# Plain float32 operands for the first token block's MLP in a fused attention, MLP and expert kernel

## The chip, the cores and the metric

One core of one Trainium2 chip runs the whole program. The metric is the device time of one execution in microseconds. Engines are named as in the profile: PE multiplies, PEld is its weight load, DVE, ACT and POOL work element by element, SP issues the transfers.

## What is computed

The reference joins three layers (cut to what matters):

```
x  = attention(q, k, v)                  # 4 x 8 heads, 576 positions, 64 features; a coarse and a banded part
h  = x @ w_in                            # 2304 x 512 @ 512 x 2048
g  = maximum(h, 0) + log1p(exp(-abs(h)))
y  = g @ w_out                           # 2048 x 512
e  = argmax(y @ w_gate + modality_bias)  # one of 8 experts for each token
out = gate * (maximum(y @ w1[e], 0) @ w2[e])
```

All of it is float32 in the reference; `w_in` and `w_out` arrive as float64 bits. The change concerns the lines of `h`, `g` and `y` for the first 384 of 2304 tokens.

## The kernel before

The tokens are cut into six blocks of 384 (`TB`, `NB`). For each block the MLP goes over 16 chunks of 128 hidden features: `mlp_H` multiplies a chunk of `w_in` by the block's x (line 557), three ACT instructions and line 572 on DVE make g, and `mlp_Y` multiplies g by a chunk of `w_out` into four PSUM banks that are held for the whole block (line 588). After the six blocks the same blocks pass through the experts (lines 557 and 632).

A product is made of float32r operands in two parts, `hi` and `lo = value - hi`: `hi*hi + hi*lo + lo*hi`, three matmuls. So every operand is split: a piece of a weight by `split` (lines 464 and 465: a copy on ACT, a subtraction on POOL), x by lines 354 and 355, g by lines 573 and 574. In block 0 line 573 runs on ACT and line 574 on POOL; in the blocks after it both run on DVE.

The weights are converted from float64 bits only once, while block 0 runs: `from_f64` takes a piece of 128 x 512 through line 425 on ACT and lines 426 to 429 on DVE. There are 32 pieces, 16 of `w_in` and 16 of `w_out`; the raw bits arrive by DMA in six buffers, and SP issues a new transfer when line 429 has freed one. The attention is written in steps that are interleaved with the MLP: what block 1 needs is made while block 0 is multiplied. Its matmuls (lines 167, 208, 237, 247, 304, 329, 338) take plain float32 operands.

The order on each engine comes from a scheduler that goes by its own estimate of the times; each engine then works through its instructions strictly in that order. So an instruction on DVE that takes longer than another also holds back what stands behind it, g above all, and PE waits for g in its second product.

Of the kernel before, what the change touches and what calls it, by code (L numbers as in the profile page):

```python
# [25 lines left out]
TB = 384  # L26
# [11 lines left out]
MASKED = -1.0e9  # L38
# The float64 2.0 ** -127 has the high word 0x38000000: as a float32, this.
F64_LEAST = 2.0 ** -15  # L40
# [6 lines left out]
C0 = 3  # L47
CR = 1


@with_exitstack
def band_attention__softplus_mlp__top1_moe(
# [49 lines left out]
    def ahead(n):  # L102
        """The scheduler takes what is emitted inside as if it had been n instructions earlier."""
        return tc.high_priority(n) if n else nullcontext()
# [7 lines left out]

# [1 line left out]
    xT = {}  # L114
    od = {}

    class Down:
# [37 lines left out]
        def trans(self, i):  # L155
            """q or k of both heads, features on partitions."""
            t = apool.tile([128, S], F32, tag=("qT", "kT")[i], name="qkT", bufs=4)
            half = RT // 2
            for g in range(2):
                ps = pa("pT")  # L160
                for r in range(half):
                    if self.b < 0:
                        for h in range(2):
                            T.matmul(ps[h * D:(h + 1) * D, r * RP:(r + 1) * RP], self.raw[i][:, h, g * half + r, :],
                                     ident[:RP, :RP], start=True, stop=True)
                        continue
                    T.transpose(ps[:, r * RP:(r + 1) * RP], self.raw[i][:, g * half + r].rearrange("p h d -> p (h d)"),  # L167
                                ident[:RP, :RP])
                warm(ps)
                o = t.rearrange("m (p r) -> m r p", r=RT)[:, g * half:(g + 1) * half, :]  # L170
                x = ps[:, :half * RP].rearrange("m (r p) -> m r p", r=half)
                if i == 0:
                    A.mul(o, x, SCALE) if g or nloc[0] >= 12 else V.tensor_scalar(o, x, SCALE, None, ALU.mult)
                else:
                    (A.copy if nloc[0] < 16 else V.tensor_copy)(o, x)
            return t
# [82 lines left out]
    def warm(ps):  # L259
        """Keeps the tensor engine's clock up while the attention leaves it idle; nobody reads the columns."""  # L260
        if 4 <= nloc[0] < 12:
            for i in range(1):
                T.matmul(ps[:, 384:384 + 128], ident, ident[:, :128], start=True, stop=True)

    def pa(name):
        """A bank for the attention: while the MLP has not begun, of any of the three pools."""
        if not started[0]:
            nps[0] += 1
            if nps[0] % 2:
                return psy.tile([128, 512], F32, tag="py", name=name)  # L270
        return psa.tile([128, 512], F32, tag="pa", name=name)
# [3 lines left out]
    class Local:  # L275
# [58 lines left out]
        def st_PV(self):  # L334
# [8 lines left out]
            if blk not in xT:  # L343
                xT[blk] = xpool.tile([128, 2, CC, TB], F32R, tag="xT", name="xT")
            xf = apool.tile([128, TH // FACTOR, FACTOR], F32, tag="xf", name="xf", bufs=2)
            jd = self.j * (TH // FACTOR)
            odb = od[self.b][:, self.hp, jd:jd + TH // FACTOR].rearrange("p (g o) -> p g o", o=1)
            V.tensor_tensor(
                out=xf, in0=ps[:, :TH].rearrange("p (g r) -> p g r", r=FACTOR),
                in1=odb.to_broadcast([128, TH // FACTOR, FACTOR]), op=ALU.add)  # L350
            xf = xf.rearrange("p g r -> p (g r)")
            hi = xT[blk][:, 0, self.hp, off:off + TH]
# [21 lines left out]
    def load_after(n):  # L374
        """The loads that fit once job n has been transposed."""
        while loads and loads[0][0] <= n:
# [40 lines left out]

# [1 line left out]
    def from_f64(raw, dst, on_g):  # L419
        """float64 bits, as (low, high) pairs of int32, to float32: the exponent loses its three  # L420
        redundant bits, the mantissa is cut to 23 bits, and what is under float32's range ends under
        its least normal number, as zero does."""
        lo, hi = raw[:, :, 0], raw[:, :, 1]
# [45 lines left out]

    def split_wi(n, c):  # L470
        wis[n, c] = split(wi[:, c] if n < NB else mo["w1"][:, :, c * 128:(c + 1) * 128], "wis")

    def split_wo(n, c):
        wos[n, c] = split((wo if n < NB else mo["w2"])[:, c, :], "wos")

    load_after(-3)

# [1 line left out]
    def router_setup():  # L479
# [19 lines left out]
    def router(n):  # L499
        """Each quarter of the features has its own columns of the array; the sum over them comes after the transpose."""  # L500
        ps = psa.tile([128, 512], F32, tag="pa", name="pR")
# [30 lines left out]
    def count_others():  # L532
        """How many tokens chose each expert but the first token's, and how many in all."""
        hits = const.tile([128, E, NTT], F32, name="hits")
# [11 lines left out]

# [1 line left out]
    gst = {}  # L548
    yps = {}

    def mlp_H(n, c):
        ps = psa.tile([128, 512], F32, tag="pa", name="ph")
        wt = wis.pop((n, c))
        i = 0
        for cc in range(CC):
            for w, x in ((0, 0), (0, 1), (1, 0)):
                T.matmul(ps[:, :TB], wt[:, w, cc, :], xT[n][:, x, cc, :], start=(i == 0), stop=(i == 3 * CC - 1))  # L557
# [9 lines left out]

    def mlp_g(n, c):
        g = mlp.tile([128, 2, TB], F32R, tag="g", name="g", bufs=3)
        if n < NB:  # L570
# [10 lines left out]
    def mlp_Y(n, c):  # L581
        g, w = gst.pop((n, c)), wos.pop((n, c))
        if c == 0:
            yps[n] = [psy.tile([128, 512], F32, tag="py", name="py") for _ in range(CC)]
        for dc in range(CC):
            dsl = slice(dc * 128, (dc + 1) * 128)
            for i, (a, b) in enumerate(((0, 0), (0, 1), (1, 0))):
                T.matmul(yps[n][dc][:, :TB], w[:, a, dsl], g[:, b, :], start=(c == 0 and i == 0),  # L588
# [9 lines left out]

# [1 line left out]
    mo = {}  # L600

    def load_expert(e):
        """One expert's weights."""
        for h in range(2):
# [8 lines left out]
    def load_y(n, y=None):  # L613
        """Block n's MLP output, split, as the experts' operand."""
        if y is None:
# [7 lines left out]
    def moe_Y(n, cs, mask=None):  # L623
        """The second product for chunks cs, token tile by token tile."""
        gw = [(gst.pop((n, c)), wos.pop((n, c))) for c in cs]
# [30 lines left out]

# [1 line left out]
    if 0:  # L658
# [63 lines left out]

# [1 line left out]
    # So far every token went through the first token's expert. What chose another one is computed  # L724
    # again: for each such expert all blocks, of which its tokens' rows are kept.
    with tc.If(nc.values_load(todo[0:1, E:E + 1], min_val=0, max_val=NT) > 0):
# [48 lines left out]
```

## Time and profile before

| what | value |
|---|---|
| runs | 836.1, 836.75, 838.21 us; median 836.75 |
| profiled execution | span 836.3 us from the first to the last instruction; no other time of it is listed |
| PE busy | 789.5 us of the span, 94% |
| DVE, ACT, POOL busy | 512.4, 476.7, 522.5 us |
| mean granted clock of TensorE | 0.962 of full |

The span is read in stages. Up to about 64 us the attention of the first tokens is made and nothing of the MLP runs. Block 0's first product begins at 64.4 us. The conversions end at 196.6 us, block 0's last product at about 213.5 us, and from there on PE has hardly a gap.

### The profile page before, as it was taken

What the parts mean: (1) busy time and instruction counts of PE and PEld (TensorE: products, weight loads), DVE (VectorE), ACT (ScalarE), POOL (GpSimd) and SP (SyncE); (2) the same over time, 40 slices, a digit from 0 to 9 for tenths busy, and PEclk for the clock granted to TensorE, in tenths of its full rate; (3) what the DMA queues carried; (4) which work ended last, traced back from release to release, by engine and by line L of the source; (5) the groups of instructions that cost most, each with busy time, mean ns of one, the idle gap of its engine ahead of it and who ended that gap; (6) DMA issues with size and microseconds to landing.
All of it is one profiled execution on the core that took longest, in us unless ns stands there. A gap on an engine that the chain in (4) does not pass through costs nothing.

```text
span 836.3 us, 14455 instructions
## 1 busy us (share of the span) xinstructions
PE 789.5 (94%) x5229; PEld 718.9 (86%) x5230; DVE 512.4 (61%) x1011; ACT 476.7 (57%) x1206; POOL 522.5 (62%) x491
## 2 busy tenths in 40 slices
PE   5997887888999999999999999999999999999996
PEld 4776876776989998898989999999998899999995
DVE  6879999998597576677765566638561512222121
ACT  5756775665556664657755665646663444444342
POOL 3457757668566575666656666656666666666662
PEclk9868988989999999999999999999999999999999
DMA  9936554432220041021100010036011102001011
GB/s 171 199 84 149 175 174 127 137 100 55 74 64 5 15 113 43 13 62 39 36 1 12 11 49 1 2 110 242 1 36 42 63 14 76 1 38 38 1 39 41
DMA packets 82169, 55.49 MB, mean 66 GB/s; under 512 B 61081, under 2 KB 73899, under 8 KB 82091
## 3 DMA queue, kind: packets, MB, share of 16 engines
q1 hardware_dynamic: 82091, 54.50, 23.4%
q8 instruction: 43, 0.70, 0.3%
q14 instruction: 35, 0.29, 0.1%
HBM read 45.05 MB, written 9.44 MB: 65 GB/s over the span
## 4 chain that ended last, share of the span: by engine, by line
PE 74%; DVE 17%; ACT 3%; issue 3%; SPq 1%; DMA 1%; DVEq 0%; ACTq 0%
PE ph L557 31%; PE py L588 19%; PE py L632 12%; DVE cva L428 3%; DVE cva L427 3%; PE pO L338 2%; PE pS L304 2%; DVE cva L426 2%; PE pA L329 2%; PE pT L167 1%; DVE ga L572 1%; PE pO L247 1%; PE pA L237 1%; DVE g L573 1%; PE pS L208 1%
## 5 line engine op out<-in xcount | busy, mean ns | idle before, releaser
L557 PE MATMUL ph<-xT,wis 128*128 128x384 f32 x1152 | 234.9, 352 | 8.2 <-DVE ls L310 2.6
L588 PE MATMUL py<-g,wos 128*128 128x384 f32 x1152 | 233.8, 345 | 2.4 <-ACT g L573 1.0
L557 PEld LDWEIGHTS ph<-xT,wis 128*128 128x128 f32 x1152 | 208.5, 197 | 13.1 <-ACT cva L425 2.7
L588 PEld LDWEIGHTS py<-g,wos 128*128 128x128 f32 x1152 | 199.7, 190 | 9.3 <-issue 2.5
L465 POOL TENSOR_TENSOR wis<-wi,wis 128x512 fp32r<-128x512 f32 x96 | 129.0, 1344 | 71.0 <-ACT wis L464 62.2
L465 POOL TENSOR_TENSOR wos<-wo,wos 128x512 fp32r<-128x512 f32 x96 | 132.4, 1380 | 48.2 <-ACT wos L464 47.9
L557 PE MATMUL ph<-yT,wis 128*128 128x384 f32 x576 | 108.2, 336 | 0.0
L578 DVE SCALAR_TENSOR_TENSOR g<-ph,g 128x384 fp32r<-128x384 f32 x48 | 26.7, 557 | 131.2 <-ACT g L577 131.2
L632 PE MATMUL py<-wos,g 128*128 128x512 f32 x432 | 106.6, 392 | 0.0
L557 PEld LDWEIGHTS ph<-yT,wis 128*128 128x128 f32 x576 | 101.5, 188 | 3.5
L465 POOL TENSOR_TENSOR wos<-w2s,wos 128x512 fp32r<-128x512 f32 x48 | 63.9, 1332 | 49.4 <-ACT wos L464 49.4
L632 PEld LDWEIGHTS py<-wos,g 128*128 128x128 f32 x432 | 80.3, 188 | 15.3 <-ACT wis L464 0.6
L563 ACT ACTIVATE ga<-ph 128x384 f32<-128x384 f32 x96 | 46.7, 487 | 78.1 <-PE ph L557 76.6
L572 DVE SCALAR_TENSOR_TENSOR ga<-ph,ga 128x384 f32<-128x384 f32 x96 | 52.9, 551 | 48.4 <-ACT ga L565 47.7
L464 ACT CAST wos<-wo 128x512 fp32r<-128x512 f32 x96 | 59.2, 617 | 38.2 <-PE py L588 34.3
L465 POOL TENSOR_TENSOR wis<-w1s,wis 128x512 fp32r<-128x512 f32 x48 | 61.8, 1288 | 29.9 <-ACT wis L464 29.8
L318 ACT ACTIVATE ls<-ls,lst 128x70 f32<-128x70 f32 x144 | 49.3, 344 | 41.4 <-DVE lst L312 41.1
L574 DVE TENSOR_TENSOR g<-ga,g 128x384 fp32r<-128x384 f32 x80 | 67.8, 848 | 1.9
L464 ACT CAST wis<-wi 128x512 fp32r<-128x512 f32 x96 | 58.7, 611 | 3.8 <-DVE wi L429 3.3
L577 ACT ACTIVATE g<-ph 128x384 fp32r<-128x384 f32 x48 | 23.6, 491 | 56.5 <-PE py L632 31.7
L324 POOL TENSOR_TENSOR ls<-ls,lst 128x210 f32<-128x210 f32 x48 | 30.8, 643 | 35.0 <-DVE lst L323 23.9
L573 DVE CAST g<-ga 128x384 fp32r<-128x384 f32 x80 | 50.1, 626 | 3.7 <-PE py L588 0.5
(127 smaller groups left out, 1111.5 us busy)
## 6 DMA issues: line engine op xcount, KB each, us to landing
raw<-in_moe_w_in_dram SPq DMA_DIRECT2D x16, 512.0 KB
raw<-in_moe_w_out_dram SPq DMA_DIRECT2D x16, 512.0 KB
lv<-in_v_dram SPq DMA_DIRECT2D x72, 70.0 KB
qr<-in_q_dram SPq DMA_DIRECT2D x32, 144.0 KB
kr<-in_k_dram SPq DMA_DIRECT2D x32, 144.0 KB
vr<-in_v_dram SPq DMA_DIRECT2D x16, 288.0 KB
ydram<-y SPq DMA_DIRECT2D x12, 384.0 KB
yb<-ydram SPq DMA_DIRECT2D x6, 768.0 KB
```

Of the source, the lines that this page charges most:

```text
L318: A.activation(s[:, i, :], s[:, i, :], AF.Exp, bias=st[:, 0, i], accum_out=st[:, 1, i])
L324: G.tensor_tensor(out=s, in0=s, in1=st[:, 1].to_broadcast([128, 3, KW]), op=ALU.mult)
L464: A.copy(w[:, 0], src)
L465: G.tensor_tensor(out=w[:, 1], in0=src, in1=w[:, 0].bitcast(F32), op=ALU.subtract)
L557: T.matmul(ps[:, :TB], wt[:, w, cc, :], xT[n][:, x, cc, :], start=(i == 0), stop=(i == 3 * CC - 1))
L563: A.activation(a, ps[:, :TB], AF.Abs)
L572: V.scalar_tensor_tensor(a, ps[:, :TB], 0.0, a, ALU.max, ALU.add)
L573: (A.copy if n < 1 else V.tensor_copy)(g[:, 0, :], a)
L574: (G if n < 1 else V).tensor_tensor(out=g[:, 1, :], in0=a, in1=g[:, 0, :].bitcast(F32), op=ALU.subtract)
L578: V.scalar_tensor_tensor(g[:, 1, :], ps[:, :TB], 0.0, g[:, 0, :].bitcast(F32), ALU.max, ALU.subtract)
L588: T.matmul(yps[n][dc][:, :TB], w[:, a, dsl], g[:, b, :], start=(c == 0 and i == 0), stop=(c == NC1 - 1 and i == 2))
L632: T.matmul(yps[n][t], g[:, a, ts], w[:, b, :], start=(c == 0 and i == 0), stop=(c == NC2 - 1 and i == 2))
```

## The change

Block 0 (`blk < NATIVE`, `n < NATIVE`, with `NATIVE = 1`) keeps x, both weights and g as plain float32, and each of its products is one matmul in the program. Its x is written by the sum on DVE straight into the tile; the splits of its weights, of x and of g are not made. The conversion from float64 stays, since the converted weights serve all blocks. Blocks 1 to 5 and the experts are as before. The lines of the changed file are some 10 to 26 higher.

```diff
+NATIVE = 1
...
             if blk not in xT:
-                xT[blk] = xpool.tile([128, 2, CC, TB], F32R, tag="xT", name="xT")
-            xf = apool.tile([128, TH // FACTOR, FACTOR], F32, tag="xf", name="xf", bufs=2)
+                if blk < NATIVE:
+                    xT[blk] = xpool.tile([128, CC, TB], F32, tag="xT", name="xN")
+                else:
+                    xT[blk] = xpool.tile([128, 2, CC, TB], F32R, tag="xT", name="xT")
+            if blk < NATIVE:
+                xf = xT[blk][:, self.hp, off:off + TH].rearrange("p (g r) -> p g r", r=FACTOR)
...
+            if blk < NATIVE:
+                return
...
     def split_wi(n, c):
+        if n < NATIVE:
+            return
...
     def split_wo(n, c):
+        if n < NATIVE:
+            return
...
     def mlp_H(n, c):
...
         for cc in range(CC):
+            if n < NATIVE:
+                T.matmul(ps[:, :TB], wi[:, c, cc, :], xT[n][:, cc, :], start=(cc == 0), stop=(cc == CC - 1))
+                continue
...
     def mlp_g(n, c):
+        if n < NATIVE:
+            ps, a = gst[n, c]
+            g = mlp.tile([128, TB], F32, tag="g", name="gN", bufs=3)
+            V.scalar_tensor_tensor(g, ps[:, :TB], 0.0, a, ALU.max, ALU.add)
+            gst[n, c] = g
+            return
...
     def mlp_Y(n, c):
...
+            if n < NATIVE:
+                T.matmul(yps[n][dc][:, :TB], wo[:, c, dsl], g, start=(c == 0), stop=(c == NC1 - 1))
+                continue
```

The scheduler gives another order. On DVE, at the end of the conversions (`cva`, `wi` and `wo` are the conversion's tiles, `ga` is g before its split, `gN` the plain g of block 0), the order before is

```order
L426 TENSOR_SCALAR cva<-cva 128x512
L429 SCALAR_TENSOR_TENSOR wo<-raw,cva 128x512
L348 TENSOR_TENSOR xf<-pO,od 128x192
L310 TENSOR_TENSOR ls<-pS,mask 128x210
L427 TENSOR_SCALAR cva<-cva 128x512
L332 COPY laT<-pA 70x384
L312 TENSOR_REDUCE lst<-ls 128x3
L428 SCALAR_TENSOR_TENSOR cva<-raw,cva 128x512
L572 SCALAR_TENSOR_TENSOR ga<-ph,ga 128x384
L429 SCALAR_TENSOR_TENSOR wo<-raw,cva 128x512
```

and of the change

```order
L437 TENSOR_SCALAR cva<-cva 128x512
L439 SCALAR_TENSOR_TENSOR wi<-raw,cva 128x512
L438 SCALAR_TENSOR_TENSOR cva<-raw,cva 128x512
L439 SCALAR_TENSOR_TENSOR wo<-raw,cva 128x512
L436 TENSOR_SCALAR cva<-cva 128x512
L437 TENSOR_SCALAR cva<-cva 128x512
L438 SCALAR_TENSOR_TENSOR cva<-raw,cva 128x512
L589 SCALAR_TENSOR_TENSOR gN<-ph,ga 128x384
L439 SCALAR_TENSOR_TENSOR wo<-raw,cva 128x512
```

The last line of each is the last of the 32 conversions. Before, 15 of block 0's 16 g stand ahead of it; now 12 do, and the attention's instructions have moved behind it.

On PE, in the last third of block 0's MLP (`ph` is the first product, `py` the second), the order before is

```order
L557 MATMUL ph<-xT,wis 128x384 x12
L588 MATMUL py<-g,wos 128x384 x8
L304 MATMUL pS<-qkT 64x70 x6
L247 MATMUL pO<-daT,vs 64x144 x4
L557 MATMUL ph<-xT,wis 128x384 x2
L588 MATMUL py<-g,wos 128x384 x4
L557 MATMUL ph<-xT,wis 128x384 x10
```

and of the change, from the place where the second product follows the twelfth g,

```order
L611 MATMUL py<-gN,wo 128x384 x4
L306 MATMUL pS<-qkT 64x70 x6
L571 MATMUL ph<-xN,wi 128x384 x4
L340 MATMUL pO<-laT,lv 64x64 x6
L331 MATMUL pA<-ident,ls 70x128 x3
L611 MATMUL py<-gN,wo 128x384 x4
```

A chunk's product is four matmuls in the program instead of twelve. The second product of a chunk now stands right behind the first product of the chunk after it.

## Rows read from the trace of the kernel before

**Rows 1.** The page's first line (busy time, share of the span and instructions of each engine), and the core's span with its mean granted clock.

```profile
PE 789.5 (94%) x5229; PEld 718.9 (86%) x5230; DVE 512.4 (61%) x1011; ACT 476.7 (57%) x1206; POOL 522.5 (62%) x491
core 0: 836.3 us, clock 0.962
```

**Rows 2.** Table of stretches: from and to in us, length, then busy time of PE, PEld, DVE, ACT and POOL (with instructions), the granted clock, the DMA engines' share and GB/s.

```profile
64.40:224.00 159.60, 134.42 (x899) 117.58 (x898) 150.14 (x245) 102.26 (x273) 113.10 (x107) 0.88 0.44 126
224.00:836.30 612.30, 602.22 (x3876) 558.33 (x3874) 314.94 (x655) 333.58 (x786) 379.79 (x327) 1.00 0.13 42
60.00:200.00 140.00, 115.82 (x803) 100.79 (x804) 138.31 (x228) 92.43 (x253) 97.91 (x90) 0.89 0.48 139
```

**Rows 3.** Groups of DVE's instructions from 60 to 200 us, those of the conversion: line, operation, out<-in, shapes, count | busy us, mean ns of one | idle time before them.

```profile
L428 DVE SCALAR_TENSOR_TENSOR cva<-raw,cva 128x512 int32<-128x512 int32 x28 | 27.8, 992 | 0.2
L427 DVE TENSOR_SCALAR cva<-cva 128x512 int32<-128x512 int32 x28 | 27.1, 969 | 0.1
L426 DVE TENSOR_SCALAR cva<-cva 128x512 f32<-128x512 f32 x28 | 21.3, 759 | 0.0
L429 DVE SCALAR_TENSOR_TENSOR wo<-raw,cva 128x512 int32<-128x512 int32 x15 | 15.4, 1027 | 0.0
L429 DVE SCALAR_TENSOR_TENSOR wi<-raw,cva 128x512 int32<-128x512 int32 x13 | 11.8, 907 | 0.0
```

**Rows 4.** The same lines one by one over the whole span: count, then shortest, median and longest duration in ns, first and last start.

```profile
L426 DVE TENSOR_SCALAR cva<-cva x32: 389/424/1519, 31.4 to 188.9; 128x512 f32<-128x512 f32 x32
L427 DVE TENSOR_SCALAR cva<-cva x32: 390/466/4054, 32.3 to 190.4; 128x512 int32<-128x512 int32 x32
L428 DVE SCALAR_TENSOR_TENSOR cva<-raw,cva x32: 674/686/3077, 33.5 to 192.5; 128x512 int32<-128x512 int32 x32
L429 DVE SCALAR_TENSOR_TENSOR wi<-raw,cva x16: 674/678/1770, 34.8 to 185.3; 128x512 int32<-128x512 int32 x16
```

**Rows 5.** Timeline of DVE and POOL at two places: start, duration, engine, line; in brackets how long the engine had been idle, and what released it.

```profile
148.56 0.68 DVE L428 SCALAR_TENSOR_TENSOR cva<-raw,cva 128x512 int32<-128x512 int32 x1
...
151.52 2.26 POOL L465 TENSOR_TENSOR wos<-wo,wos 128x512 fp32r<-128x512 f32 x1 [3.17 <-ACT wos L464]
...
192.49 3.08 DVE L428 SCALAR_TENSOR_TENSOR cva<-raw,cva 128x512 int32<-128x512 int32 x1
...
192.52 1.28 POOL L465 TENSOR_TENSOR wis<-wi,wis 128x512 fp32r<-128x512 f32 x1
193.76 1.25 POOL L465 TENSOR_TENSOR wos<-wo,wos 128x512 fp32r<-128x512 f32 x1
```

**Rows 6.** Groups of POOL's instructions from 60 to 200 us, columns as in rows 3.

```profile
L465 POOL TENSOR_TENSOR wos<-wo,wos 128x512 fp32r<-128x512 f32 x15 | 22.3, 1484 | 7.4 <-ACT wos L464 7.2 <-POOL ls L324 0.2
L465 POOL TENSOR_TENSOR wis<-wi,wis 128x512 fp32r<-128x512 f32 x15 | 21.8, 1456 | 12.7 <-ACT wis L464 8.3 <-ACT g L573 2.2 <-PE pT L167 2.2
L574 POOL TENSOR_TENSOR g<-ga,g 128x384 fp32r<-128x384 f32 x15 | 20.0, 1330 | 2.1 <-ACT g L573 2.1
...
L355 POOL TENSOR_TENSOR xT<-xf,xT 128x192 fp32r<-128x192 f32 x11 | 8.6, 786 | 8.6 <-DVE xT L354 4.4 <-DVE lst L322 4.2
```

**Rows 7.** Timeline of DVE: where block 0's stretch of conversions begins, and its last conversion with what follows.

```profile
66.11 1.60 DVE L322 TENSOR_SCALAR lst<-lst 128x3 f32<-128x3 f32 x1
...
195.96 0.68 DVE L429 SCALAR_TENSOR_TENSOR wo<-raw,cva 128x512 int32<-128x512 int32 x1
196.56 0.15 DVE L322 TENSOR_SCALAR lst<-lst 128x3 f32<-128x3 f32 x1
```

**Rows 8.** Timeline of PE in a stretch at full clock. A row merges what follows each other; the next row's start is where the next matmul was fed in.

```profile
300.50 0.90 PE L208 MATMUL pS<-dkT,dbd 128*96 128x144 f32 x6
301.33 0.72 PE L247 MATMUL pO<-daT,vs 72*64 72x144 f32 x8
...
302.25 2.34 PE L588 MATMUL py<-g,wos 128*128 128x384 f32 x12
304.43 2.25 PE L557 MATMUL ph<-xT,wis 128*128 128x384 f32 x12
306.60 0.58 PE L304 MATMUL pS<-qkT 64*64 64x70 f32 x12
```

**Rows 9.** Single records: plain float32 weight loads of line 208 and matmuls of line 503 (shortest, median, longest ns), and from the page's costliest groups the float32r matmuls and weight loads of line 557 (busy us, mean ns).

```profile
L208 PEld LDWEIGHTS pS<-dkT,dbd x96: 159/163/285, 11.1 to 429.6; 128*96 128x96 f32 x96
L503 PE MATMUL pR<-y,wg x48: 486/498/510, 234.1 to 645.0; 128*32 128x384 f32 x48
L557 PEld LDWEIGHTS ph<-xT,wis 128*128 128x128 f32 x1152 | 208.5, 197 | 13.1 <-ACT cva L425 2.7
L557 PE MATMUL ph<-yT,wis 128*128 128x384 f32 x576 | 108.2, 336 | 0.0
```

**Rows 10.** Groups of PE's matmuls from 64.4 to 224.0 us, columns as in rows 3: the two MLP products, then the first and the last of the nine other groups.

```profile
L557 PE MATMUL ph<-xT,wis 128*128 128x384 f32 x240 | 60.6, 404 | 7.9 <-DVE ls L310 2.6 <-DVE laT L332 2.0 <-DVE ga L572 1.0
L588 PE MATMUL py<-g,wos 128*128 128x384 f32 x215 | 47.9, 360 | 1.9 <-ACT g L573 1.0 <-POOL g L574 0.8
L338 PE MATMUL pO<-laT,lv 70*64 70x64 f32 x144 | 10.1, 246 | 0.8 <-DVE laT L332 0.8
...
L488 PE MATMUL pI<-ident,idf 18*128 18x18 f32 x1 | 0.2, 231 | 0.0
```

**Rows 11.** Timeline of PE where block 0's last second product ends.

```profile
211.82 1.86 PE L588 MATMUL py<-g,wos 128*128 128x384 f32 x8
213.52 0.41 PE L167 MATMUL pT<-ident,kr 96*128 96x96 f32 x3
```

More of the change, by code (lines that the diff above doesn't have):

```diff
@@ L343, in st_PV @@
             if blk not in xT:
-                xT[blk] = xpool.tile([128, 2, CC, TB], F32R, tag="xT", name="xT")
-            xf = apool.tile([128, TH // FACTOR, FACTOR], F32, tag="xf", name="xf", bufs=2)
+                if blk < NATIVE:
[4 more added lines that the diff above has]
+                xf = xT[blk][:, self.hp, off:off + TH].rearrange("p (g r) -> p g r", r=FACTOR)
+            else:
+                xf = apool.tile([128, TH // FACTOR, FACTOR], F32, tag="xf", name="xf", bufs=2)
             jd = self.j * (TH // FACTOR)
@@ L552, in mlp_H @@
         ps = psa.tile([128, 512], F32, tag="pa", name="ph")
-        wt = wis.pop((n, c))
+        wt = None if n < NATIVE else wis.pop((n, c))
         i = 0
         for cc in range(CC):
+            if n < NATIVE:
+                T.matmul(ps[:, :TB], wi[:, c, cc, :], xT[n][:, cc, :], start=(cc == 0), stop=(cc == CC - 1))
+                continue
             for w, x in ((0, 0), (0, 1), (1, 0)):
@@ L581, in mlp_Y @@
     def mlp_Y(n, c):
-        g, w = gst.pop((n, c)), wos.pop((n, c))
+        g, w = gst.pop((n, c)), None if n < NATIVE else wos.pop((n, c))
         if c == 0:
```

## The prediction

> **What bounds the kernel now.** I read the page's shares first, then a table of stretches, then the two engines that matter stretch by stretch. PE is 94% busy and its granted clock is 0.96 of full over the span [rows 1], so the kernel as a whole is a TensorE kernel. But the table of stretches shows two different kernels [rows 2]. From 224.0 us on PE is busy 602.22 of 612.3 us at a granted clock of 1.00: there only less TensorE work would help, and the change touches nothing there. From 64.4 to 224.0 us, where block 0's MLP runs, PE is busy 134.42 of 159.6 us, so 25.2 us are idle, and its granted clock is 0.88. DVE is busy 138.31 of the 140 us from 60 to 200: in block 0's stage DVE sets the pace.
>
> What DVE does there is the conversion of the weights: four instructions for each of 28 pieces between 60 and 200 us [rows 3]. The reader is to compare their means with their minima [rows 3, 4]: line 427 takes 969 ns on average and 390 at least, line 426 takes 759 and 389, line 428 takes 992 and 674, line 429 takes 1027 and 907 with a minimum of about 674. The excess is 28 x (0.579 + 0.370 + 0.318) + 15 x 0.353 + 13 x 0.233 = 35.5 + 5.3 + 3.0 = 43.8 us. The timeline says whose it is [rows 5]: one line 428 runs from 192.49 for 3.08 us while POOL works through two splits, 192.52 to 193.80 and 193.76 to 195.01, and ends 0.56 us after the second; at 148.56, with POOL idle until 151.52, it takes 0.68 us. So DVE's excess is time behind POOL, and POOL's work there is mostly the splits that the change removes.
>
> The Trainium skill ("SBUF — State Buffer", the list under "Reading the diagram") calls this an exclusive lock on a port pair that DVE and GpSimd share: the second to start is blocked until the first has finished. By that rule alone a line 428 could lose one split at most and take 0.68 + 1.3 = 2.0 us; the trace has 3.08, two splits long, so here the rule is too mild, and I go by the rows.
>
> **The change, part by part.**
>
> *POOL and ACT lose work.* Block 0's splits go (16 of w_in, 16 of w_out) with 16 residuals of g and 8 of x. Between 60 and 200 us the two kinds of split and the residual of g cost POOL 22.3 + 21.8 + 20.0 = 64.1 us of its 97.9 [rows 2, 6]; the block 0 part of line 355 is about 5 x 0.786 = 3.9 more. What stays is 97.9 - 68.0 = 29.9, plus the first splits of block 1 and some that I miscount, say 34 us, or 0.34 of the old. ACT loses 32 casts and 16 copies; it is busy 102.26 of the stage's 159.6 us [rows 2], so that is worth nothing by itself.
>
> *DVE gets faster without losing work.* It keeps every conversion and the scalar_tensor_tensor of line 572. If the excess goes with POOL's busy time, 43.8 x 0.66 = 29 us go. From 66.1 us, where the stretch begins, to 196.6, the end of the last conversion [rows 7], DVE took 130.5 us; it would take 101, and end near 167. The new order also puts that last conversion behind the twelfth g, where the old one has it behind the fifteenth: fewer attention instructions stand before it, and small instructions are stretched too (line 322 took 1.60 us at 66.11 [rows 7] against 0.15 at 196.56 [rows 7]). With both counted I get 89 us, an end near 155. So 155 to 167.
>
> *PE gets more work.* A product of block 0 was 3 float32r matmuls and becomes one plain float32 matmul, of which a trace shows two records: line 503 issues 24 of these and has 48 [rows 9]. The float32r price is a pace, since matmuls are pipelined: 12 of line 588 from 302.25 to 304.43 and 12 of line 557 to 306.60 [rows 8] make 181.5 ns each. Before has no plain float32 matmul of 384 columns on the full array, so I bound it. Line 503 has 384 columns but 32-column weights: its record lasts 498 ns where a float32r record of the same columns lasts 336 [rows 9], which is one more pass of some 160 ns (384 columns at 2.4 GHz). Two passes are 320, the lower end. Line 208 is nearest in kind, plain float32 with 96-column weights: six records from 300.50 to 301.33 [rows 8], 138 ns for 144 columns, where two passes are 120. In proportion that is 369 ns for 384 columns, the upper end; as a fixed excess of 18 ns it is 338. The float32r pace also has a fixed excess (181.5 against 160), so I take 340 and keep 320 to 369 for the range. Block 0 then takes 16 x 8 x 2 = 256 records x 0.340 = 87.0 us for 384 x 0.1815 = 69.7: PE work grows by **17.3 us**, between 12.2 and 24.8.
>
> *Sum.* The stage's 159.6 us hold 240 + 215 = 455 MLP matmuls [rows 10], 82.6 us at full pace, and attention matmuls that are busy for 40.9 us (nine groups, 10.1 for line 338 down to 0.2 for line 488 [rows 10]). The other 36.1 us are PE waiting, or running at half clock. New: 82.6 + 17.3 + 40.9 = 140.8, if DVE never holds PE. The 40.9 hold slow-clock time and pipeline ends, which I leave in as an allowance for the wait at the start of the stage, so the gain is 159.6 - 140.8 = 18.8 us. Does DVE keep up? After the twelfth g, PE still has 32 native products x 0.68, 12 float32r matmuls and about 5 us of attention, 29 us together. With DVE there at 155 to 167 the block could end at 184 to 196; before, its last product ended at 213.5 [rows 11], with 4 us more of the following block's work done. DVE therefore allows a gain of 13 to 25 us. PE and DVE are nearly balanced, and two balanced queues never mesh quite; I take 2 off: **16.8 us**.
>
> *Edits that I cost at nothing.* Weight loads: SP issues a raw piece when line 429 frees a buffer, and DMA is 0.44 busy in the stage [rows 2]; the same bytes in some 0.8 of the time make that about 0.6. Were that cover gone, DVE would wait at line 428. Reordering: in the new order a second product stands one chunk behind its first product instead of two to three; between the two stand another chunk's products, 8 x 0.68 = 5.4 us, against the three ACT instructions and one on DVE that make g, about 2.1 us.
>
> From the profiled execution's 836.3 us that gives 819.5; its span is 0.45 us under the median of the runs, 836.75, so I say **820**.
>
> **The rivals.**
>
> *The weight loads come into the open (slower).* A plain float32 product needs two weight loads. If they did not run under the matmul before them, a record would cost 320 + 197 ns [rows 9] = 517, and block 0 132 us: PE work +63, and 159.6 becomes about 187, some 27 us slower, **864**. It decides from a price at which 82.6 - 69.7 + 40.9 + 256 p reaches 159.6, that is p = 413 ns. Against it: line 208's load lasts 163 ns and its pace is 138, not 283, so its loads are hidden. For it: no row has the full 128 columns. The Trainium skill ("TensorE: Matmul & The Clock Gate", "The mechanism" of Part 3) speaks for it: a weight load overlaps a running matmul only where the row groups differ, and here they are the same. By that, with the page's 107 ns for 128 columns, a record would be 427 ns by estimate and the stage about 163 us, no gain. The rows of line 208 contradict it. **0.12.**
>
> *The stall moves instead of going (no change).* PE's 36.1 us of waiting and low clock would shrink only by as much as its work grows, 17.3: if DVE's excess follows not POOL's busy time but the number of POOL instructions that meet it, and what stays on POOL is short (line 355, 786 ns [rows 6]) but still meets the conversions. Then about 15 of 44 us go, DVE ends near 182 and block 0 near 211: **835 to 837**. For it: the excess per instruction differs much. Against: line 465 is the longest that DVE meets, and 30 of them go. **0.09.**
>
> *POOL's removal frees DVE fully (faster still).* With no excess left and 320 ns a record PE alone bounds: 82.6 + 12.2 + 32 (attention at full clock) + 5 = 132, a gain of 28, **809**. The clock helps it, since it falls after PE's waits and those shrink. **0.17.**
>
> The forecast case, 812 to 830, has the remaining **0.62**.
>
> **How the numbers follow.** A measurement of this kernel can tell about 0.3% from no change, 2.5 us. Faster: 0.62 + 0.17 = 0.79, less 0.01 for the edge; same 0.09; slower 0.13. The range runs from the fastest case with a little room to just under no change, 807 to 834; left out are the slower rival, half of the unchanged one, and little below.
>
> **What would show it.** Right: between 66 and 160 us lines 426 to 429 near 0.4, 0.4, 0.7 and 0.7 us; DVE under 95% busy in that stretch and PE over 93%; the last conversion at 155 to 167 us; native records about 340 ns apart at full clock; the end of block 0's last product (213.5 us before) near 193; after it a profile like the old one, shifted. Wrong: native records over 413 ns apart; means of the conversion lines still near 0.9 us; or PE idle as long as before, waiting for DVE behind g.

## The result and the profile after

The changed kernel takes **814.71 us** (median of 4 runs, 810.96 to 818.24), the kernel before, run beside it, 836.42 us (4 runs, 834.73 to 838.21). The ratio is **0.9734**, 95% interval 0.9695 to 0.9774: 2.7% faster. The forecast was 820 us, in a range from 807 to 834. The profiled execution took 816.7 us, of which the span is 814.8. In what follows a slow run, such as one of 1920 us of the kernel with ACT's work back, counts in the median of its kernel but not in the ratio. Lines of the conversion have moved by ten: 426 to 429 are 436 to 439 now. Block 0's products are lines 571 (first) and 611 (second), those of the other blocks 574 and 614; the splits of line 465 stand in line 475.

First the page's shares and the core's clock, then the stretches (columns as in [rows 2]).

```profile
PE 788.8 (97%) x5101; PEld 690.1 (85%) x5102; DVE 469.0 (58%) x1008; ACT 452.8 (56%) x1153; POOL 449.6 (55%) x435
core 0: 814.8 us, clock 0.979
```

```profile
60.00:200.00 140.00, 134.76 (x822) 88.76 (x820) 109.30 (x253) 82.75 (x241) 45.18 (x58) 0.99 0.51 147
64.40:199.70 135.30, 130.11 (x766) 85.03 (x765) 105.45 (x242) 78.35 (x224) 43.34 (x56) 0.99 0.50 145
66.00:155.50 89.50, 84.31 (x475) 51.96 (x474) 83.82 (x184) 55.40 (x153) 26.97 (x33) 0.98 0.65 190
199.70:814.80 615.10, 605.55 (x3886) 561.62 (x3883) 317.19 (x659) 335.08 (x789) 379.26 (x327) 0.99 0.13 42
220.00:240.00 20.00, 17.83 (x116) 16.74 (x115) 14.19 (x28) 11.31 (x31) 10.76 (x11) 0.83 0.05 12
```

Against [rows 1, 2] the reader is to see three things. PE's busy time over the span is the same (788.8 for 789.5), and the time in which PE stands still fell from 46.8 to 26.0 us, nearly the whole gain. That is not because the new products cost nothing: by the pace shown below they cost some 17 us more, and the higher granted clock of block 0's stage, 0.99 for 0.88, makes up for them (from 64.40 us to equal work PE is busy 130.11 us in place of 134.42). From 60 to 200 us DVE's 138.31 us became 109.30, POOL's 97.91 became 45.18, and PE went from 115.82 busy at a granted clock of 0.89 to 134.76 at 0.99. And the work that the kernel before had done at 224.0 us (48 first-product matmuls of block 1 and its first 23 or 24 second-product ones) is done at 199.7: 24.3 us sooner. The rest of the program takes 615.1 us in place of 612.3, so 2.8 us of it are given back.

The conversion's instructions from 60 to 200 us (columns as in [rows 3]):

```profile
L438 DVE SCALAR_TENSOR_TENSOR cva<-raw,cva 128x512 int32<-128x512 int32 x28 | 20.6, 735 | 0.2
L437 DVE TENSOR_SCALAR cva<-cva 128x512 int32<-128x512 int32 x28 | 16.3, 581 | 0.1
L436 DVE TENSOR_SCALAR cva<-cva 128x512 f32<-128x512 f32 x28 | 13.3, 474 | 4.2 <-ACT cva L435 4.2
L439 DVE SCALAR_TENSOR_TENSOR wo<-raw,cva 128x512 int32<-128x512 int32 x15 | 11.2, 746 | 0.1
L439 DVE SCALAR_TENSOR_TENSOR wi<-raw,cva 128x512 int32<-128x512 int32 x13 | 9.2, 711 | 0.0
```

The counts are those of [rows 3]; the sum fell from 103.4 to 70.6 us. At the minima of [rows 4] the same instructions take 28 x (0.389 + 0.390 + 0.674 + 0.674) = 59.6, so the excess fell from 43.8 to 11.0 us. Line 436 now waits 4.2 us for ACT, where line 426 never waited. Of this 3.8 us are one wait, and behind it stands a transfer: ACT's line 435, which comes before line 436, had itself waited for a raw piece of `w_in`.

```profile
82.97 0.68 ACT L435 ACTIVATE cva<-raw 128x512 f32<-128x512 f32 x1 [3.86 <-DMA raw<-in_moe_w_in_dram]
83.68 0.43 DVE L436 TENSOR_SCALAR cva<-cva 128x512 f32<-128x512 f32 x1 [3.81 <-ACT cva L435]
```

That DVE's excess is time beside POOL can be counted over all 112 instructions of [rows 3] (28 each of four lines), from the start times and durations of both engines. Before, 27 of them run while POOL is idle; none of these is more than 29 ns over its minimum, and together they lose 0.3 us. The 85 that meet a POOL instruction lose the other 43.5. After, 74 meet none and lose 1.2 us; 38 meet one and lose 9.9. On POOL the two rows of line 475 are what is left of the splits, now block 1's:

```profile
L326 POOL TENSOR_TENSOR ls<-ls,lst 128x210 f32<-128x210 f32 x14 | 9.0, 645 | 25.2 <-DVE lst L325 22.4 <-ACT cva L435 2.9
...
L232 POOL TENSOR_TENSOR de<-de,dsm 96x432 f32<-96x432 f32 x4 | 6.1, 1521 | 23.0 <-DVE dsm L231 9.7 <-DVE xT L364 7.6 <-ACT od L254 5.7
L475 POOL TENSOR_TENSOR wis<-wi,wis 128x512 fp32r<-128x512 f32 x3 | 3.9, 1289 | 4.0 <-ACT wis L474 4.0
L475 POOL TENSOR_TENSOR wos<-wo,wos 128x512 fp32r<-128x512 f32 x3 | 3.8, 1277 | 3.0 <-ACT wos L474 3.0
```

What PE pays for a plain float32 product: the single records of line 571 (count, then shortest, median and longest ns, first and last start), and a timeline of PE, where the next row's start is the pace.

```profile
L571 PEld LDWEIGHTS ph<-xN,wi x128: 186/190/337, 64.4 to 175.4; 128*128 128x128 f32 x128
L571 PE MATMUL ph<-xN,wi x128: 486/486/980, 64.5 to 175.7; 128*128 128x384 f32 x128
```

```profile
132.86 2.77 PE L571 MATMUL ph<-xN,wi 128*128 128x384 f32 x8
135.56 0.59 PE L306 MATMUL pS<-qkT 64*64 64x70 f32 x12
...
183.09 2.85 PE L611 MATMUL py<-gN,wo 128*128 128x384 f32 x8
185.86 0.58 PE L306 MATMUL pS<-qkT 64*64 64x70 f32 x12
...
222.64 0.58 PE L306 MATMUL pS<-qkT 64*64 64x70 f32 x12 [1.00 <-DVE qkT L177]
224.31 1.18 PE L340 MATMUL pO<-laT,lv 70*64 70x64 f32 x12 [1.09 <-DVE qkT L177]
```

Eight records (four products) take 135.56 - 132.86 = 2.70 us, 337.5 ns each. A load alone lasts 190 ns and does not show in that pace. Block 0's last product ends at 185.9; before it ended at 213.5 [rows 11]. The last two rows are where some of the gain is given back: PE waits 2.1 us for DVE's copies of qkT. The wait alone is not what is lost, since 24.3 us later in the kernel before, at the same place in the work, PE is idle for 1.7 us too (below). What differs is the granted clock in that stretch, 0.83 after and 1.00 before; why it fell there only after the change, no run shows.

```profile
244.30:264.30 20.00, 18.31 (x137) 17.30 (x136) 14.45 (x31) 14.44 (x39) 13.89 (x14) 1.00 0.05 12
```

### The profile page after: what moved, and what is told of

The parts are those of the page before. It is cut to its first block, busy times and chain, and to the rows that moved or that the text cites. A ratio compares the mean times of both kernels' runs of the same rounds, so it can differ in the third digit from the quotient of the medians.

```text
span 814.8 us, 14060 instructions
## 1 busy us (share of the span) xinstructions
PE 788.8 (97%) x5101; PEld 690.1 (85%) x5102; DVE 469.0 (58%) x1008; ACT 452.8 (56%) x1153; POOL 449.6 (55%) x435
## 4 chain that ended last, share of the span: by engine, by line
PE 85%; DVE 6%; ACT 3%; DMA 2%; SPq 1%; issue 1%; POOL 0%; DVEq 0%; POOLq 0%; ACTq 0%
PE ph L574 32%; PE py L614 19%; PE py L658 12%; PE ph L571 4%; PE py L611 4%; PE pO L340 3%; PE pS L306 3%; PE pA L331 2%; PE pO L249 1%; PE pT L169 1%; PE pS L210 1%; PE pA L239 1%; DVE g L596 1%; SPq L136 1%; DMA qr<-in_q_dram 1%
## 5 line engine op out<-in xcount | busy, mean ns | idle before, releaser
L614 PE MATMUL py<-g,wos 128*128 128x384 f32 x960 | 192.4, 344 | 0.0
L574 PE MATMUL ph<-xT,wis 128*128 128x384 f32 x960 | 184.3, 339 | 0.3 <-ACT qkT L175 0.2
L614 PEld LDWEIGHTS py<-g,wos 128*128 128x128 f32 x960 | 166.9, 190 | 4.9 <-issue 1.7
L574 PEld LDWEIGHTS ph<-xT,wis 128*128 128x128 f32 x960 | 166.8, 188 | 2.5 <-issue 0.8
L475 POOL TENSOR_TENSOR wis<-wi,wis 128x512 fp32r<-128x512 f32 x80 | 107.0, 1338 | 60.6 <-ACT wis L474 55.0
L475 POOL TENSOR_TENSOR wos<-wo,wos 128x512 fp32r<-128x512 f32 x80 | 107.7, 1347 | 41.4 <-ACT wos L474 41.3
L580 ACT ACTIVATE ga<-ph 128x384 f32<-128x384 f32 x96 | 46.8, 487 | 93.7 <-PE ph L574 76.3
L475 POOL TENSOR_TENSOR wis<-w1s,wis 128x512 fp32r<-128x512 f32 x48 | 61.8, 1288 | 30.5 <-ACT wis L474 30.4
L595 DVE SCALAR_TENSOR_TENSOR ga<-ph,ga 128x384 f32<-128x384 f32 x80 | 44.1, 551 | 49.6 <-ACT ga L582 49.1
L474 ACT CAST wos<-wo 128x512 fp32r<-128x512 f32 x80 | 49.5, 619 | 36.3 <-PE py L614 36.0
L597 DVE TENSOR_TENSOR g<-ga,g 128x384 fp32r<-128x384 f32 x80 | 65.7, 821 | 2.0
L582 ACT ACTIVATE ga<-ga 128x384 f32<-128x384 f32 x96 | 50.4, 525 | 1.9
```

What stands on the lines that cost most here:

```text
L474: A.copy(w[:, 0], src)
L475: G.tensor_tensor(out=w[:, 1], in0=src, in1=w[:, 0].bitcast(F32), op=ALU.subtract)
L580: A.activation(a, ps[:, :TB], AF.Abs)
L582: A.activation(a, a, AF.Ln, bias=1.0)
L595: V.scalar_tensor_tensor(a, ps[:, :TB], 0.0, a, ALU.max, ALU.add)
L597: (G if n < 1 else V).tensor_tensor(out=g[:, 1, :], in0=a, in1=g[:, 0, :].bitcast(F32), op=ALU.subtract)
```

## The experiments

After the result my theory was that the gain is DVE's relief from POOL's splits, and that the plain float32 products themselves cost PE time. The rivals: the products, the new order or ACT's lighter load bring the gain, and POOL hardly counts. Each ratio is against the kernel before on the same chip. The scheduler orders each kernel anew, so the orders are alike but not the same: in the kernels with plain products 11 or 12 of block 0's 16 g stand ahead of the last conversion, in the kernel before and the one without residuals 15.

**POOL's work given back, products still plain.** The POOL instructions of the splits (in split_wi, and in the same way in split_wo) and of g's residual return, and nobody reads what they write:

```diff
+    def pool_only(src, tag):
+        w = mlp.tile([128, 2] + list(src.shape)[1:], F32R, tag=tag, name=tag, bufs=2)
+        G.tensor_tensor(out=w[:, 1], in0=src, in1=src, op=ALU.subtract)
...
         if n < NATIVE:
+            pool_only(wi[:, c], "wis")
...
-            g = mlp.tile([128, TB], F32, tag="g", name="gN", bufs=3)
+            g2 = mlp.tile([128, 2, TB], F32, tag="g", name="gN", bufs=3)
+            g = g2[:, 0, :]
             V.scalar_tensor_tensor(g, ps[:, :TB], 0.0, a, ALU.max, ALU.add)
+            G.tensor_tensor(out=g2[:, 1, :], in0=a, in1=g, op=ALU.subtract)
```

> The changed kernel with POOL's work of block 0 put back, with no reader: each of the 32 weight pieces is subtracted from itself on POOL into the unused second half of a split tile (128x512), and the residual of g is written to an unused half of g's tile (16 of 128x384). ACT's casts stay out and the products stay plain float32. Theory (the gain is DVE's time behind POOL): the four conversion lines go back to means near 0.75 to 1.0 us, the last conversion moves from 155.5 to about 185 to 195 us, and with PE's 17 us more of work the time is 833 to 848 us, at or above the kernel before. Rival (the products no longer wait for a split operand): nothing waits for POOL here, so 811 to 819 us, as the changed kernel. Rival (ACT was the one relieved): the same 811 to 819.

Measured: 846.37 us, ratio 1.0172 (1.0115 to 1.0228), within the 833 to 848 us expected. It is slower than the kernel before, some 34 us slower than the changed one on the same chip with ACT's work back (below). The rows of its conversion (60 to 200 us) and its stretch of conversions:

```profile
L438 DVE SCALAR_TENSOR_TENSOR cva<-raw,cva 128x512 int32<-128x512 int32 x28 | 26.9, 962 | 0.2
L436 DVE TENSOR_SCALAR cva<-cva 128x512 f32<-128x512 f32 x28 | 21.1, 753 | 6.6 <-ACT cva L435 6.4
L437 DVE TENSOR_SCALAR cva<-cva 128x512 int32<-128x512 int32 x28 | 19.3, 688 | 0.1
```

```profile
66.00:183.50 117.50, 97.26 (x486) 57.36 (x485) 109.36 (x180) 57.01 (x155) 75.74 (x71) 0.91 0.49 145
```

The means of lines 438 and 436 are back near those of [rows 3], that of line 437 (688 ns for 969) about halfway, the clock is back at 0.91, and the same conversions end at 183.5 in place of 155.5, just ahead of the expected 185 to 195. They still end 13 us sooner than before, and yet the kernel is slower, because the last conversion now stands behind the eleventh g and not the fifteenth: block 0's last product ends 32.3 us after it (at 215.7 us), where before it ended 17.0 us after it. So the plain products with their new order are a loss without the relief: those rivals fall.

**ACT's work given back.** As above, with ACT's cast in place of POOL's instruction:

```diff
+    def act_only(src, tag):
+        w = mlp.tile([128, 2] + list(src.shape)[1:], F32R, tag=tag, name=tag, bufs=2)
+        A.copy(w[:, 0], src)
```

> The changed kernel with ACT's 32 weight casts of block 0 put back, with no reader (128x512 each, about 0.61 us, 19.6 us in all). POOL stays free, the products stay plain float32. Theory (DVE behind POOL): ACT has room, 811 to 819 us as the changed kernel. Rival (ACT was the one relieved): most of the 21.7 us gain is lost again, 826 to 836 us.

Measured: 812.31 us, ratio 0.976 (0.9684 to 0.9835), not to be told from the changed kernel and within the 811 to 819 us expected. ACT's 32 casts are worth nothing that shows beside the noise of some 6 us, as the prediction said.

**The relief without the plain products.** The kernel before, without block 0's second parts (lo is n > 0): its three float32r matmuls remain, all of them on the first parts. What it leaves out are the products `hi*lo` and `lo*hi`; in their place it adds `hi*hi` twice more, so block 0's output is not only without the residuals' share, as the expectation says, but each of its products is about three times too large. The matmuls, the conversions and the later work are as many as before (1152 and 1152 for the two MLP products, 432 in line 632's place).

```diff
             for w, x in ((0, 0), (0, 1), (1, 0)):
+                w, x = (w, x) if n > 0 else (0, 0)
...
-            G.tensor_tensor(out=w[:, 1], in0=src, in1=w[:, 0].bitcast(F32), op=ALU.subtract)
+            if lo:
+                G.tensor_tensor(out=w[:, 1], in0=src, in1=w[:, 0].bitcast(F32), op=ALU.subtract)
```

> The kernel before with block 0's residuals left out: no subtraction on POOL for its weights, its x or its g, and the first (hi) part stands in for the second in the three float32r matmuls, so PE issues the same 384 float32r matmuls and ACT the same casts. The output of block 0 therefore lacks the residuals' share. Theory (DVE behind POOL): DVE's conversions end near 150 to 160 us as in the changed kernel, and PE has 17 us less to do than there, so the block ends at or before the changed kernel's 186 us: 800 to 813 us. Rival (it is the plain float32 form of the products, fewer instructions on PE and no split chain on ACT, that gains): 832 to 838 us, as before. Rival (the products waited for their splits): between the two, since ACT's casts stay: 815 to 830.

Measured: 793.7 us, ratio 0.9561 (0.9499 to 0.9623), faster than even the theory's 800 to 813 us, and far from both rivals. From 60 to 200 us (lines 428 and 430 here are 427 and 429 of before):

```profile
L428 DVE TENSOR_SCALAR cva<-cva 128x512 int32<-128x512 int32 x28 | 14.7, 526 | 0.1
L430 DVE SCALAR_TENSOR_TENSOR wo<-raw,cva 128x512 int32<-128x512 int32 x15 | 10.9, 724 | 0.0
```

```profile
60.00:200.00 140.00, 133.67 (x1006) 122.42 (x1007) 121.94 (x275) 109.24 (x295) 61.34 (x71) 0.98 0.51 145
```

The conversion is relieved as in the changed kernel, but only 8.8 us of PE's work follow the last conversion, so block 0 ends at 163.7 us. In parts of 836.4 us: the relief alone gives 0.0439 x 836.4 = 36.7 us, the plain products with their order cost 0.0172 x 836.4 = 14.4, and both together gave 0.0266 x 836.4 = 22.2. The parts add up, 36.7 - 14.4 = 22.3, though each is known to some 5 us only by its interval.

**Block 1 plain as well**, where PE is the bound:

```diff
-NATIVE = 1
+NATIVE = 2
```

> The changed kernel with block 1 on plain float32 operands too (NATIVE = 2). In block 1 PE is busy without a gap and DVE converts nothing. Theory (the gain is DVE's in block 0, and plain float32 is the dearer product): block 1 costs 256 records x 0.337 - 384 x 0.1815 = 16.6 us more, 828 to 834 us. Rival (plain float32 operands relieve the kernel wherever splits are): a second gain of 5 to 20 us, 795 to 810 us.

Measured: 828.72 us, ratio 0.993 (0.9885 to 0.9974), in the theory's range. On the same chip its median is 16.4 us over that of the run with ACT's work back (0.017 apart in ratio, which is 14 us). The price by pace is 256 x 0.3375 - 384 x 0.1815 = 16.7. A stretch of block 1, with the same stretch of the changed kernel above it, and the records of line 571:

```profile
186.00:245.00 59.00, 56.83 (x396) 53.46 (x395) 41.77 (x89) 34.25 (x90) 34.54 (x35) 0.94 0.20 52
186.00:245.00 59.00, 59.00 (x303) 36.62 (x302) 23.93 (x67) 23.44 (x68) 10.19 (x16) 1.00 0.20 52
```

```profile
L571 PE MATMUL ph<-xN,wi x256: 486/486/847, 64.0 to 275.4; 128*128 128x384 f32 x128
```

PE is busy in all of the 59 us while POOL falls from 34.54 to 10.19: where PE is the bound, taking work off POOL buys little, and the plain product is paid in full.

**Two thirds of POOL's work given back** (the first experiment without the residual of g):

```diff
-            G.tensor_tensor(out=g2[:, 1, :], in0=a, in1=g, op=ALU.subtract)
```

> The run with POOL's work put back, but only the 32 weight subtractions (128x512), without the 16 residuals of g. POOL then has 41 to 44 of the 64 us back. Theory in the form that DVE loses in proportion to POOL's busy time: two thirds of the 34 us between the run with POOL's work back and the one with ACT's, so 20 to 26 us over the changed kernel, 0.997 to 1.006 of before. Rival (what holds the kernel back there is the residual of g, which occupies g's three buffers until POOL is done, and not DVE): the time falls back to within 5 us of the changed kernel, 0.973 to 0.980.

Measured: 831.1 us, ratio 1.0004 (0.9965 to 1.0043). The ratio lies in the theory's range, but the distance to the changed kernel on the same chip does not: 15.6 us by the medians (14 by the ratios), below the 20 to 26 expected, and above the rival's 5. So the weights' subtractions alone cost most of what was forecast, and the residual of g more than its share. In the profiles the time from block 0's first product to the last conversion is 106.3 us here, 117.5 with all of POOL's work back and 91.0 in the changed kernel; behind that conversion all three need 30.5 to 32.3 us. So the residual of g, too, costs its time mostly while DVE converts. In neither profile does the DVE instruction that makes g wait for POOL, as it would if g's buffers were what is short; with all of POOL's work back it is ACT that waits for POOL, 6.8 us in all.

```profile
L438 DVE SCALAR_TENSOR_TENSOR cva<-raw,cva 128x512 int32<-128x512 int32 x28 | 26.2, 936 | 0.1
L437 DVE TENSOR_SCALAR cva<-cva 128x512 int32<-128x512 int32 x28 | 17.7, 633 | 0.1
L436 DVE TENSOR_SCALAR cva<-cva 128x512 f32<-128x512 f32 x28 | 16.9, 604 | 4.5 <-ACT cva L435 4.5
```

```profile
66.00:175.60 109.60, 94.19 (x484) 57.29 (x485) 101.69 (x185) 58.38 (x162) 62.08 (x65) 0.89 0.54 162
```

**Back to float32r once the conversion is over.** If POOL's splits only cost while DVE converts, then block 0's last second products should be float32r again, with 4 x (0.675 - 0.5445) = 0.52 us of PE saved by each chunk. From chunk 8 (FY = 8), and from chunk 11, with the test replaced in split_wo, mlp_g and mlp_Y:

```diff
+FH, FY = 16, 8
+def plain(n, c, first):
+    return n < NATIVE and c < first
...
-        if n < NATIVE:
+        if plain(n, c, FY):
```

> The changed kernel, but block 0's second product takes float32r operands again from chunk 8 on (w_out and g split, 8 chunks), when DVE is ahead with its conversions; the first product stays plain. PE saves 8 x (8 x 0.3375 - 12 x 0.1815) = 4.2 us; POOL gets 8 splits and 8 residuals back, some 18 us, about half of it while DVE still converts, which by the first four runs costs DVE 4 us that it has in hand. Theory (PE bounds the second half of block 0): 3 to 4 us less than the changed kernel, 0.965 to 0.972 of before. Rival (any POOL work in block 0 comes back through DVE): the same as the changed kernel or up to 5 us slower, 0.974 to 0.982.

> As the run before, but from chunk 11 on (5 chunks), when the conversions have ended. Theory: 5 x 0.52 = 2.6 us less than the changed kernel, 0.968 to 0.974 of before, with no cost on DVE. Rival: no difference that can be told, 0.973 to 0.976.

> The changed kernel itself, for comparison on the same chip as the next three: 0.970 to 0.978 of the kernel before.

Measured on one chip: 809.86 us (0.9763, 0.9734 to 0.9793) from chunk 8, 807.31 (0.9737, 0.9686 to 0.9788) from chunk 11, and 815.51 (0.9834, 0.9781 to 0.9887) for the changed kernel again, which is outside its expected 0.970 to 0.978. By the ratios chunk 8 falls in the rival's range and chunk 11 where both ranges meet; beside the changed kernel of the same chip both look like more than the expected gain, so chunk 11 and the changed kernel were run a second time:

> Block 0's second product on float32r operands from chunk 11 on, once more. Theory (PE bounds the second half of block 0, 2.6 us less work): 1 to 6 us under the changed kernel of this set, with a mean over both sets of 0.4 to 0.9% under it. Rival (the 8 us of the set before were the difference of two draws): no more than 1 us either way in this set.

> The changed kernel once more, beside the next run on the same chip: 0.972 to 0.985 of the kernel before.

Measured: 811.53 us (0.9723, 0.9662 to 0.9785) and 812.96 (0.9722, 0.9664 to 0.9781): no difference by the ratios and 1.4 us by the medians, where the theory had 1 to 6 us and the rival at most 1. The changed kernel's own ratios over three sets are 0.9734, 0.9834 and 0.9722, so their spread is wider than the 2.6 us in question, and whether the late splits make the whole kernel faster stays open. The traces show the two terms themselves. From the last conversion to block 0's last product the changed kernel takes 30.5, 30.7 and 30.8 us in its three profiles; chunk 11 takes 28.1 and 28.0, which is the forecast 2.6 less, and chunk 8 takes 26.6, which is 4.1 less where 4.2 were forecast. What chunk 8 saves there it pays ahead of the last conversion, where DVE's excess is 14.3 us for 11.0; from chunk 11 on the splits cost DVE nothing that shows:

```profile
66.00:157.60 91.60, 87.95 (x492) 54.96 (x491) 85.40 (x188) 58.26 (x164) 33.37 (x37) 0.97 0.64 191
```

## Why the prediction was right, and where its sizes were off

The same measures for the kernels show the mechanism. "Excess" is the busy time of the conversion's lines from 60 to 200 us, less 59.6; POOL's busy time and the granted clock are those of the stretch from 66 us to the last conversion's end. When block 0's first product begins differs from one execution to the next (64.5, 56.1 and 64.8 us in three profiles of the changed kernel), so it stands beside the ends. The row of the kernel before for that stretch is

```profile
66.00:196.60 130.60, 107.21 (x727) 93.48 (x726) 129.79 (x204) 84.25 (x223) 92.06 (x83) 0.88 0.47 137
```

| kernel | first product of block 0 begins | conversion ends | last product of block 0 ends | POOL busy until the conversion ends | DVE's excess | per us of POOL | granted clock | ratio |
|---|---|---|---|---|---|---|---|---|
| before | 64.4 | 196.6 | 213.7 | 92.1 | 43.8 | 0.48 | 0.88 | 1 |
| POOL's work back | 65.9 | 183.5 | 215.7 | 75.7 | 31.9 | 0.42 | 0.91 | 1.0172 |
| two thirds back | 69.3 | 175.6 | 206.6 | 62.1 | 23.1 | 0.37 | 0.89 | 1.0004 |
| float32r from chunk 8 | 58.2 | 155.2 | 181.8 | 39.5 | 14.3 | 0.36 | 0.98 | 0.9763 |
| float32r from chunk 11 | 68.0 | 157.6 | 185.7 | 33.4 | 9.8 | 0.29 | 0.97 | 0.9737, 0.9723 |
| changed | 64.5 | 155.5 | 185.9 | 27.0 | 11.0 | 0.41 | 0.98 | 0.9734 |
| relief without plain products | 54.5 | 154.9 | 163.7 | 25.6 | 9.5 | 0.37 | 0.99 | 0.9561 |
| ACT's work back | 57.3 | 150.1 | 180.2 | 25.1 | 11.3 | 0.45 | 0.98 | 0.976 |

- **DVE's relief: right in kind, a little better than forecast.** The prediction scaled the excess with POOL's busy time, to 15 us; 11.0 remain. Its 34 us for POOL's remainder in a fixed stretch came out as 45.18, because six splits of block 1 (7.7 us) now fall before 200 us and some instructions grew longer. By its own rule that would have left 43.8 x 45.18 / 97.91 = 20.2 us. But only 27.0 of those lie before the conversion's end, and 43.8 x 27.0 / 92.1 = 12.8. POOL's time has to be counted while DVE converts: a faster conversion also meets less of POOL. That the 15 came so close is in part luck: the rest of POOL's work was counted too small, and over too long a stretch.
- **The means** were forecast near 0.4, 0.4, 0.7 and 0.7 us and came out at 0.47, 0.58, 0.74 and 0.71 to 0.75. The last conversion ended at 155.5, at the early end of 155 to 167. The early end stood on a figure of 89 us for the new order and the small instructions, for which the prediction shows no working; the trace has 89.4. DVE's other instructions between 66 us and the last conversion's end take 83.82 - 70.6 = 13.2 us in place of 129.79 - 103.4 = 26.4; 4.9 us of what that saves go again, as DVE is idle for 5.7 us there in place of 0.8.
- **The plain product's price: right.** 337.5 ns a record against 340. The rival in which the weight loads come into the open needed 413 ns; the loads last 190 ns on the full array and stay hidden. The Trainium skill's sentence ("TensorE: Matmul & The Clock Gate", "The mechanism" of Part 3) that a load overlaps only where row groups differ is contradicted here by the rows of line 571; the same section also lets a load into the background weight buffer run ahead of matmuls, and with that the rows agree.
- **Weight loads by DMA: right in the share, but not free.** Its share is 0.65 between 66 and 155.5 us (about 0.6 forecast). The prediction put its cost at nothing; one transfer came late, and DVE stood still for 3.8 us behind ACT's line 435 (the rows at 82.97 and 83.68 us), where before it never waited.
- **The path behind the last conversion: right.** The prediction counted 29 us of PE's work after the twelfth g. In the changed kernel block 0's last product ends 30.5 us after the last conversion, and in the other kernels with plain products throughout block 0 it ends 30.0 to 32.7 us after it. So the conversion's end sets the block's end. With 185.9 us it came at the early side of the forecast 184 to 196, and ahead of the 193 named as a sign.
- **PE's stage: the term of the sum that was mis-sized.** The block's MLP matmuls cost 256 x 0.3375 + 72 x 0.1815 = 99.5 us, as forecast (82.6 + 17.3 = 99.9). For attention and the waits that cannot be avoided the prediction left 40.9, and 2 for two queues that do not mesh; the stage to equal work took 135.3, so both together were 35.8 and not 42.9. The 40.9 were sums of records, taken from a stretch at a clock of 0.88. The same nine groups sum to 36.4 us after, at a clock of 0.99; records overlap, so even that is more than they take, since PE's idle time of 5.2 us (130.11 busy of 135.3) is also in the 35.8. Those 5.2 us are what was left of waits and of queues that do not mesh.
- **What comes later: not foreseen.** 2.8 us are given back behind 199.7; the stretch found for it is 220 to 240 us, at a granted clock of 0.83. So the profiles differ by 24.3 - 2.8 = 21.5 us where the forecast had 16.8: the stage gained 7.5 us more than forecast, and a loss that was not in the sum hid part of the difference.
- **The rivals.** "The stall moves" is refuted: what stays on POOL (645 to 1521 ns an instruction) meets the conversions and costs 11 us, not 29. "Freed fully" did not come about in its condition, since 11 us of excess remain, but its consequence nearly did: PE is busy 96% of the stage.

## What to carry to other kernels

Where DVE is the bound and its instructions last longer than their own minimum, look for what POOL does in the same microseconds, and price that work by the DVE time it stretches (here 0.3 to 0.5 us per us of POOL) and not by POOL's idle share. Work that goes off POOL may then be worth some PE time: here 36.7 us for 14.4, while the same exchange in the next block, where PE is the bound, lost 14 to 16. An order that puts the slow engine's last conversion earlier also leaves more of PE's work behind it (17.0 us before, 30.5 after), so an earlier end of the conversion is not yet as much of a gain. Sums of busy times from a stretch at a low clock are too large a price for the same work at full clock.

## What the runs showed of the hardware that was not expected

- The stretching goes both ways. Of the 62 conversion instructions of before that start while a POOL instruction runs, 53 end after it, and 9 run through in their minimum time. Then it is POOL that takes longer. In the kernel before, the split at 151.52 takes 2.26 us [rows 5], where its median over the span is 1.29, while two conversion instructions take their minima:

```profile
151.57 0.68 DVE L429 SCALAR_TENSOR_TENSOR wi<-raw,cva 128x512 int32<-128x512 int32 x1
152.26 0.39 DVE L427 TENSOR_SCALAR cva<-cva 128x512 int32<-128x512 int32 x1
```

  With POOL's work back, one such instruction takes 4.67 us beside a dense run of DVE instructions, six of the conversion among them at 0.41 and 0.68 us; right after it line 436 takes 4.62 us beside POOL's next ones:

```profile
92.73 4.67 POOL L482 TENSOR_TENSOR wos<-wo 128x512 fp32r<-128x512 f32 x1 [1.56 <-DVE dsm L231]
97.87 4.62 DVE L436 TENSOR_SCALAR cva<-cva 128x512 f32<-128x512 f32 x1
```

  Which of the two engines waits, and for how many instructions of the other, no run settles. POOL's normalisation of 96x432 elements, four instructions from 60 to 200 us, took 1020 ns on average before and 1521 after, 1898 with late splits, although POOL had less to do; why is not settled either. The row of before:

```profile
L230 POOL TENSOR_TENSOR de<-de,dsm 96x432 f32<-96x432 f32 x4 | 4.1, 1020 | 2.7 <-DVE dsm L229 1.7 <-ACT cva L425 1.0
```

- A DVE instruction that waits out a single POOL instruction is seen alone after the change, in a timeline of the two engines:

```profile
150.07 1.66 POOL L150 TENSOR_TENSOR vr<-vr 72x512 f32<-72x512 f32 x1 [1.62 <-DMA vr<-in_v_dram]
150.63 1.65 DVE L439 SCALAR_TENSOR_TENSOR wo<-raw,cva 128x512 int32<-128x512 int32 x1
...
154.81 0.68 DVE L439 SCALAR_TENSOR_TENSOR wo<-raw,cva 128x512 int32<-128x512 int32 x1
```

  Line 439 takes 1.65 us beside line 150 and 0.68 alone; it ends 0.55 us after line 150 does. That is one instruction waited out, as the Trainium skill ("SBUF — State Buffer", "Reading the diagram") has it; the 3.08 us of [rows 5] were two.
- TensorE's granted clock goes with DVE's stalls: 0.88 to 0.91 in the three kernels of the table whose conversion is stretched, 0.97 to 0.99 in the others. In those three PE stands idle for 15 to 23 us of the stretch before the conversion's end, in the changed kernel for 5. The plain products do not decide it: with POOL's work back they are in use and the clock is 0.91. How much of the time is DVE's stall and how much the clock, no run separates.
